# Attention with a feed-forward block: early transfers ahead of constants, batch 1's normalised rows by a SyncE transpose, and one buffer for the last outputs

## The chip, the cores and the metric

The kernel runs on one core of one Trainium2 chip. The metric is the device time of an execution in microseconds; the time of the kernel before is the median of three runs. A core has five engines that work side by side, each with its own queue of instructions in a fixed order: TensorE (PE, matrix products and transposes; PEld is its loading of weights), VectorE (DVE), ScalarE (ACT), GpSimd (POOL) and SyncE (SP, which mainly issues transfers). A transfer (DMA) is issued by an engine's queue, done by 16 shared DMA engines, and lands some microseconds later. An instruction that needs another's result waits on a semaphore, and all that stands behind it in its engine's queue waits with it.

## The reference

```python
scale = 1 / sqrt(D)                                  # B, H, S, D = 8, 8, 576, 64
scores = scale * q @ k.T
cum = cumsum(maximum(s, 0), axis=-1)
bias = -(cum[:, :, :, None] - cum[:, :, None, :])
scores = where(causal, -1e9, scores + minimum(bias, 0))
attn = softmax(scores);  o = attn @ v
x = o.transpose(0, 2, 1, 3).reshape(B, S, H * D)     # (8, 576, 512)
xn = (x - mean(x)) / sqrt(var(x) + 1e-6) * g_ln
out = x + relu(xn @ w_ch1) @ w_ch2                   # 512 -> 2048 -> 512
```

Every batch goes through causal attention with a bias made of running sums, a normalisation of its rows, and a feed-forward block (MLP) whose result is added to the attention's.

## The kernel before

**Tiles.** The 576 rows of a batch are four row tiles of 128 and a tail of 64 (NF = 4, NT = 5, TL = 64). The bias is carried by four more rows beside the 64 of q and k (KA = 68), which hold the running sums in three bf16 pieces (c3). The tails of two batches share one tile (xm, xnm, xTm) and are multiplied at the very end of the kernel (mixed_units).

**Order.** The whole kernel is scheduled by hand: instructions stand on each engine in the order in which the Python code emits them. The string PLAN (L942) lists steps by name (table STEPS) for heads 0 to 17; a loop (L973) emits heads 18 to 63. Batch 0 goes tile by tile (tile_tr T, tile_evac e, tile_scores S, tile_pv V, tile_norm N); later heads by scores (s), scores_d (d), pv (v), pv_norm (n). A head number runs over all batches: head 8 is the first of batch 1, head 18 the third of batch 2. Between the attention's steps, units of an earlier batch's MLP are taken from `queue` by run_units (U and u in the PLAN): mlp1 (one block of 128 hidden columns: four products into ph, then a relu into hT) and mlp2 (a quarter of a row tile: four products into py, and after the fourth quarter yo = py · rstd + x and the output's transfer). run_units(n, True) has the relu of its first unit on VectorE, the others go to ScalarE. The PSUM pool ps_m, with two buffers, holds trt, ph and py; yo lies in a pool of three (yop).

**Inputs.** The layouts of q and k are made in three ways. Batch 0: row tiles loaded by GpSimd's queue with a cast to bf16 (ld_cast_tile, L148) and transposed on TensorE (T). Groups of two heads, called pairs 4 to 11 (heads 8 to 23): ld_cast_pair (L152) loads kp and qp, tr_kind (L276, Q.k.g and Q.q.g in the PLAN) transposes them on TensorE, evac_half (E) copies them to kq. From head 24 on: rows are loaded by SyncE (ld_rows, L170), cast by GpSimd (cast_rows, L178) and transposed by a SyncE transfer (tr_rows, L188). aug (L212, L214) writes the bias rows of a kq buffer with four small SyncE transfers. v is loaded with a cast by GpSimd's queue (ld_cast_v, L160) into v_bf[0] or v_bf[1], by the batch's parity; beside a head's 64 columns each buffer has a column of ones, which gives the softmax's sum. The weights come in four chunks each (ld_w1 L200, ld_w2 L203).

**GpSimd's queue at the start.** It holds, in this order (L638 to L682): ident and maskT; k, q and v of tile 1 with gb (the norm's gain) behind them, of tiles 2 and 3, v of tile 3; w1 chunk 0; pair 4; the tails' k, q and v; constants of kq[2]; w1 chunk 1; constants of v_bf and er, among them the ones columns of v_bf[1] (L666, L667); pair 5; w1 chunk 2; two constants of cT; the five v loads of batch 1; pair 6; w1 chunk 3; w2 chunk 0; pairs 7 and 8; w2 chunk 1. A load that GpSimd issues also waits until the eighth before it has landed. Behind these come w2 chunks 2 and 3 and the causal selects (L346) of heads 10 and up.

**Normalisation and transposition.** ln_xn(b, t) (step l) makes xn of a row tile on VectorE, and with a batch's last tile also rstd. The MLP needs xn transposed (xT). For batches 0 and 1, ln_tr (L527) does this by four TensorE transposes for each tile and a copy from PSUM. From batch 2 on, ln_tr_dma does it with one SyncE transposing transfer for the four full tiles (L516) and one for the tail tile (L512). In the loop, `end` is the head after which the next batch's units enter the queue, and the number of units per head is spread over what remains.

**Which lines matter.** The stalls in the prediction are read at L276 (transposes of pairs), L539 (mlp1), L547 (a relu on VectorE), L557 (mlp2), L566 (yo).

Of the kernel before, what the change touches and what calls it, by code (L numbers as in the profile page):

```python
# [19 lines left out]
def kernel(  # L20
# [11 lines left out]
    nc = tc.nc  # L32
    B, H, S, D = q.shape
# [14 lines left out]
    NG = BH // G  # L48
    NPE = 6
    NM = 10  # L50
    NXD = 2
    KT = 96
    QT = 6
    QP = S // QT
# [99 lines left out]
    def ld_cast_pair(g):  # L154
        ld_cast("k", g)
        ld_cast("q", g)

    def ld_cast_v(b, t):
        pn = P if t < NF else TL
        nc.gpsimd.dma_start(  # L160
            out=v_bf[b % 2][:pn, t, :, 0:D],
            in_=v[b, :, t * P : t * P + pn, :].rearrange("h s d -> s h d"),
        )
# [34 lines left out]
    def ld_w1(c):  # L198
        sl = slice(c * 512, (c + 1) * 512)
        nc.gpsimd.dma_start(out=w1_bf[:, :, sl], in_=w1_r[:, :, sl])  # L200
# [272 lines left out]
    def ln_xn(b, t):  # L473
        tiles = x_tiles(b)
        if t >= len(tiles):
            return
        if b == 0:
            nc.vector.tensor_scalar(
                out=mean0[:, t : t + 1],
                in0=sum0[:, t, 0:1],  # L480
                scalar1=sum0[:, t, 1:2],
                scalar2=1.0 / Dm,
                op0=ALU.add,
                op1=ALU.mult,
            )
# [16 lines left out]
        xns[b, t] = xn  # L502
        if b > 0 and t == len(tiles) - 1:
            ln_rstd(b)
# [44 lines left out]
            nc.scalar.activation(out=hT[:, fb, :], in_=ph, func=ACT.Relu)  # L549

    py = {}

    def mlp2(t, quarter, x, rs, dst, c0=0, c1=512):
        if quarter == 0:
            py[t] = ps_m.tile([P, Dm], F32, name="py", tag="m")[:, 0 : c1 - c0]
        for fb in range(quarter * 4, quarter * 4 + 4):
            nc.tensor.matmul(  # L557
                py[t],
                lhsT=hT[:, fb, t * P : (t + 1) * P],
                rhs=w2_bf[:, fb, c0:c1],  # L560
                start=(fb == 0),
                stop=(fb == FB - 1),
            )
        if quarter == 3:
            yo = yop.tile([P, Dm], F32, name="yo", tag="yo")[:, 0 : c1 - c0]
            nc.vector.scalar_tensor_tensor(  # L566
                out=yo, in0=py[t], scalar=rs, in1=x[:, c0:c1], op0=ALU.mult, op1=ALU.add
            )
            dst(yo, c0, c1)
# [48 lines left out]
    )  # L618
    nc.sync.dma_start(out=c_in, in_=s.rearrange("b h s -> (b h) s"))
    ld_tile("k", 0, nc.sync)  # L620

    nc.vector.memset(zeros.bitcast(F32), 0.0)
    nc.vector.memset(warm, 0.0)
# [5 lines left out]
    nc.vector.memset(rowb[:, :, H : 2 * H, D + 1 : KA], 1.0)  # L629
    nc.vector.memset(v_bf[0][:, 0:NF, :, D : D + 1], 1.0)  # L630
    nc.vector.memset(v_bf[0][0:TL, NF, :, D : D + 1], 1.0)
    for i in range(2):
        nc.vector.memset(kq[i][0:KA, 0, :, S:SP], 0.0)
    nc.vector.memset(eight, 1.0 / scale)
    nc.vector.memset(mhalf, -0.5)
    nc.vector.memset(c3[BH:KT], 0.0)
    nc.vector.memset(rowb[TL:KT, NF], 0.0)
    make_identity(nc, ident)  # L638
    nc.gpsimd.memset(maskT, 0.0)
    nc.gpsimd.affine_select(  # L640
        out=maskT,
        in_=maskT,
        compare_op=ALU.is_ge,
        fill=-1.0e30,
        base=0,
        pattern=[[1, P]],
        channel_multiplier=-1,
    )
    for t in range(1, NF):
        ld_cast_tile("k", t)  # L650
        ld_cast_tile("q", t)
        ld_cast_v(0, t - 1)
        if t == 1:
            nc.gpsimd.dma_start(out=gb, in_=moe_g_ln.partition_broadcast(P))
    ld_cast_v(0, NF - 1)
    ld_w1(0)
    ld_cast_pair(4)
    ld_cast_tile("k", NF)
    ld_cast_tile("q", NF)
    ld_cast_v(0, NF)  # L660

    nc.gpsimd.memset(kq[2][:, :, :, S:SP], 0.0)
    for u, two in ((0, -1.0058441162109375), (1, 1.0019378662109375)):
        nc.gpsimd.memset(kq[2][D:P, u].bitcast(F32)[:, :, 0 : S // 2], two)  # L664
    ld_w1(1)
    nc.gpsimd.memset(v_bf[1][:, 0:NF, :, D : D + 1], 1.0)  # L666
    nc.gpsimd.memset(v_bf[1][0:TL, NF, :, D : D + 1], 1.0)  # L667
    for i in range(2):
        nc.gpsimd.memset(v_bf[i][TL:P, NF, :, :], 0.0)
    nc.gpsimd.memset(er[:, :, OD:EW], 0.0)  # L670
    ld_cast_pair(5)
    ld_w1(2)
    nc.gpsimd.memset(cT[:, :, 0, :, 0], -1.0)
    nc.gpsimd.memset(cT[:, :, 1, :, 1:4], 1.0)
    for t in range(NT):
        ld_cast_v(1, t)
    ld_cast_pair(6)
    ld_w1(3)
    ld_w2(0)
    ld_cast_pair(7)  # L680
# [200 lines left out]
    def pv_next():  # L881
        pb, ph_ = pend.pop(0)
        pv(pb, ph_)
        pv_norm(pb, ph_)
        if ph_ in (3, 5, 7):
            ln_stats(pb, ph_ // 2 - 1)
        if ph_ == 7:
            ln_open(pb)
# [24 lines left out]
        "M": piece,  # L913
        "r": piece_relu,
        "W": lambda n: keep_warm(n),
        "Sk": last_scores,
        "xk": last_exp,
        "relur": lambda: nc.scalar.activation(
# [21 lines left out]
    }  # L940

    PLAN = """  # L942
        relu.0 scan.0 relur hi.0 scan.1 sub.0 hi.1 ck sub.1 mid.0 W.4 mid.1 lo.0 tc.0 bc.0 W.2
        cq T.0.0 scan.2 lo.1 hi.2 e.0.0:D T.0.1 W.2 e.0.1:D sub.2 tc.1 S.0.0.0 x.0.0.0 S.0.1.0
        bc.1 V.0.0 T.1.1 mid.2 N.0.0 x.0.1.0 T.1.0 V.0.1 e.1.1:D S.1.1.0 lo.2 e.1.0:A tc.2 bc.2
# [27 lines left out]
    for n in range(2 * H + 2, BH):  # L973
        b, h = n // H, n % H
        pre(n)

        end = next(m for m in [8 * i + (3 if i <= NXD else 4) for i in range(2, B)] + [BH + 3] if m >= n)
        nu = -(-len(queue) // (end - n + 1)) - 2
        if h % G == 0 and n > 4 * NPE:
            run_units(2)  # L980
            nu -= 2
        scores(b, h)
        run_units(1, True)
        if h % 2 == 0:
            scores_d(b, h // 2)
        post(n)
        run_units(1)
        pv_next()
        pend.append((b, h))
        if b <= NXD:  # L990
            if n == 2 * H + 2:
                for t in range(3, NT):
                    ln_xn(1, t)
            for t in {1: (0, 1, 2), 2: (3, 4)}.get(h, ()) if b > 2 else ():
                ln_xn(b - 1, t)
                if t in (1, 2, 4):
                    run_units(1)
                    nu -= 1
            for t in {2: (0, 1), 3: (2, 3, 4)}.get(h, ()):
                ln_tr(b - 1, t, "act" if b == 2 else "dve")  # L1000
                if t not in (1, 4) and nu > 0:
                    run_units(1)
                    nu -= 1
# [12 lines left out]
        if n == end:  # L1016
            run_units(len(queue))
            queue += batch_units(b - 1)
# [42 lines left out]
```

## Time and profile before

| what | value |
| --- | --- |
| median of three runs | 353.77 us (353.52, 353.77, 355.91) |
| profiled execution, its own time | 354.29 us |
| span of the profiled execution | 352.6 us, 8239 instructions |
| granted TensorE clock | 1.0 |
| TensorE busy | 344.4 us, 98% of the span |
| VectorE, ScalarE, GpSimd busy | 192.2, 190.4, 162.0 us |
| chain that ended last | TensorE 81%, DMA 7%, GpSimd 6% |
| HBM traffic | 37.11 MB read, 9.44 MB written |

The span is what the profiler saw from the first instruction to the last; the execution's own time is 1.7 us longer. In a timeline a row has the start, the duration, the engine, the line of the code, the operation with its tiles (out<-in) and how many instructions the row sums up. A bracket at its end tells how long the engine was idle before it, and whose event ended that. In the page's slices each digit is the busy share of a fortieth of the span, in tenths. In a list of transfers the last number is the median time from issue to landing.

### The profile page before, as it was taken

The numbers are of one execution on the slowest core, as the hardware profiler recorded it, in microseconds if no ns is written. First come the engines' busy times: TensorE is split into PE (matmuls) and PEld (weight loads), VectorE is DVE, ScalarE is ACT, GpSimd is POOL, SyncE is SP. The second block draws the span as 40 slices with busy tenths as digits, with TensorE's granted clock in tenths as the row PEclk, the third lists the DMA queues.
The fourth block names the chain that finished last, engine by engine and source line by source line (L and its number), as shares of the span: only waits on it lengthen the run. The fifth ranks groups of instructions, "written<-read, shape, count | busy, mean of one in ns | idle before, by whom it ended". The sixth has DMA issues, their size and how long they took to land.

```text
span 352.6 us, 8239 instructions
## 1 busy us (share of the span) xinstructions
PE 344.4 (98%) x3110; PEld 196.1 (56%) x3110; DVE 192.2 (55%) x519; ACT 190.4 (54%) x365; POOL 162.0 (46%) x334
## 2 busy tenths in 40 slices
PE   7999999999999999999999999999999999999995
PEld 3898666655555555555555555555555544444444
DVE  7788688964366537562655458443844582113112
ACT  4799798977635673367526662576347403402500
POOL 9996587284455736383756365445521010000000
PEclk9999999999999999999999999999999999999999
DMA  9999999899998999999999999999830033011012
GB/s 150 170 164 150 201 204 129 144 176 143 187 188 132 196 210 178 210 198 176 188 199 205 198 180 171 203 160 200 148 108 0 3 81 112 2 59 59 3 41 79
DMA packets 169160, 50.31 MB, mean 143 GB/s; under 512 B 156896, under 2 KB 164512, under 8 KB 169120
## 3 DMA queue, kind: packets, MB, share of 16 engines
q1 hardware_dynamic: 115168, 36.54, 56.0%
q0 software_dynamic: 52432, 12.46, 41.1%
q10 hardware_dynamic: 1520, 0.79, 0.9%
q8 instruction: 24, 0.39, 0.5%
q14 instruction: 16, 0.13, 0.1%
HBM read 37.11 MB, written 9.44 MB: 132 GB/s over the span
## 4 chain that ended last, share of the span: by engine, by line
PE 81%; DMA 7%; POOL 6%; DVE 2%; issue 1%; SPq 1%; POOLq 0%; DVEq 0%
PE ph L539 32%; PE py L557 32%; PE pot L404 7%; DMA w_bf<-in_moe_w_ch_dram 5%; PE sc L326 3%; PE sb L326 3%; PE sa L326 3%; POOL rowb L148 2%; DMA rowtmp<-in_q_dram 2%; POOL v_bf L160 1%; PE trqk L276 1%; DMA out_dram<-yo 1%; DVE yo L566 1%; SPq L170 1%; POOL kq L664 1%
## 5 line engine op out<-in xcount | busy, mean ns | idle before, releaser
L557 PE MATMUL py<-w_bf,hT 128*128 128x512 bf16 (+2 forms) x608 | 133.6, 368 | 0.0
L539 PE MATMUL ph<-xT,w_bf 128*128 128x512 bf16 x480 | 112.5, 379 | 0.7 <-DMA w_bf<-in_moe_w_ch_dram 0.7
L549 ACT ACTIVATE hT<-ph 128x512 bf16<-128x512 f32 x102 | 60.8, 598 | 73.2 <-PE ph L539 73.2
L557 PEld LDWEIGHTS <-hT 128*128 128x128 bf16 x608 | 54.3, 98 | 52.7
L539 PEld LDWEIGHTS <-w_bf 128*128 128x128 bf16 x544 | 49.5, 98 | 51.3 <-issue 0.8
L337 ACT ACTIVATE er<-sa 128x512 bf16<-128x512 f32 x56 | 33.4, 597 | 59.4 <-PE sa L326 53.0
L346 POOL TENSOR_SCALAR_AFFINE_SELECT er<-er 128x256 bf16<-128x256 bf16 x108 | 44.3, 430 | 35.5 <-ACT er L337 34.7
L547 DVE TENSOR_SCALAR hT<-ph 128x512 bf16<-128x512 f32 x34 | 23.5, 692 | 58.0 <-PE ph L539 50.0
L566 DVE SCALAR_TENSOR_TENSOR yo<-py,rstd,xb 128x512 f32<-128x512 f32 x32 | 23.9, 748 | 35.8 <-PE py L557 34.5
L404 PEld LDWEIGHTS <-er 128*128 128x128 bf16 x840 | 32.9, 98 | 13.1 <-POOL er L346 0.9
L326 PEld LDWEIGHTS <-kq 68*128 68x128 bf16 x400 | 28.5, 97 | 19.8
L160 POOL DMA_DIRECT2D v_bf<-in_v_dram x40 | 34.6, 872 | 2.5 <-PE pot L404 1.8
L404 PE MATMUL pot<-v_bf,er 128*128 128x65 bf16 x840 | 34.9, 194 | 0.4 <-POOL er L346 0.4
L337 ACT ACTIVATE er<-sc 128x512 bf16<-128x512 f32 x56 | 34.1, 610 | 0.0
L337 ACT ACTIVATE er<-sb 128x512 bf16<-128x512 f32 x56 | 33.5, 597 | 0.0
L178 POOL CAST rowb<-rowtmp 128x512 bf16<-128x512 f32 (+1 forms) x25 | 15.3, 610 | 34.4 <-DMA rowtmp<-in_k_dram 14.9
L416 DVE RECIPROCAL rinv<-pot 128x5 f32<-128x5 f32 x56 | 10.8, 192 | 36.9 <-PE pot L404 36.8
L178 POOL CAST kq<-rowtmp 128x512 bf16<-128x512 f32 (+1 forms) x25 | 15.4, 616 | 30.9 <-DMA rowtmp<-in_q_dram 27.5
L418 DVE TENSOR_TENSOR xb<-pot,rinv 128x256 f32<-128x256 f32 x56 | 23.8, 425 | 1.9
L494 DVE SCALAR_TENSOR_TENSOR xn<-xb,mv,gb 128x512 bf16<-128x512 f32 x28 | 22.9, 818 | 1.0
L448 DVE BATCH_NORM_STATS2 stats<-xb 128x6 f32<-128x128 f32 (+1 forms) x84 | 21.9, 320 | 0.3
L326 PE MATMUL sc<-kq 68*128 68x256 bf16 (+1 forms) x192 | 21.7, 228 | 0.0
(118 smaller groups left out, 354.4 us busy)
## 6 DMA issues: line engine op xcount, KB each, us to landing
out_dram<-yo SPq DMA_DIRECT2D x32, 256.0 KB
rowtmp<-in_k_dram SPq DMA_DIRECT2D x40, 128.0 KB
rowtmp<-in_q_dram SPq DMA_DIRECT2D x40, 128.0 KB
v_bf<-in_v_dram POOLq DMA_DIRECT2D x32, 128.0 KB, 5.6
w_bf<-in_moe_w_ch_dram POOLq DMA_DIRECT2D x8, 512.0 KB, 9.7
kp<-in_k_dram POOLq DMA_DIRECT2D x8, 144.0 KB, 7.9
qp<-in_q_dram POOLq DMA_DIRECT2D x8, 144.0 KB, 7.9
rowtmp<-in_k_dram SPq DMA_DIRECT2D x10, 64.0 KB
```

Source lines behind the costliest of these rows:

```text
L160: nc.gpsimd.dma_start(out=v_bf[b % 2][:pn, t, :, 0:D], in_=v[b, :, t * P : t * P + pn, :].rearrange("h s d -> s h d"),)
L178: nc.gpsimd.tensor_copy(out=rows[gam % 2][0:pn, t, :, :, 0:D], in_=loaded.pop(("rows", gam, t))[0:pn])
L326: nc.tensor.matmul(a[:, c + a0 - q0 : c + a1 - q0], lhsT=k_cols(b, h, kb), rhs=cols, start=True, stop=not (pe_mask and diag),)
L337: nc.scalar.activation(out=e[:, o : o + 512], in_=a, func=ACT.Exp, scale=scale)
L346: nc.gpsimd.affine_select(out=two, in_=two, compare_op=ALU.is_ge, fill=0.0, base=0, pattern=[[0, 2], [1, P]], channel_multiplier=-1,)
L404: nc.tensor.matmul(pot[:, t, :], lhsT=e[:, o : o + P], rhs=vv[:, kb, h, :], start=(kb == 0), stop=(kb == last),)
L418: nc.vector.tensor_tensor(out=xb[b][:, :, hs], in0=pot[:, 0:NF, 0:D], in1=rinv[:, 0:NF].unsqueeze(2).to_broadcast([P, NF, D]), op=ALU.mult,)
L539: nc.tensor.matmul(ph, lhsT=w1_bf[:, kd, fb * P : (fb + 1) * P], rhs=xT[:, :, kd, :], start=(kd == 0), stop=(kd == KD - 1),)
L547: nc.vector.tensor_scalar_max(out=hT[:, fb, :], in0=ph, scalar1=0.0)
L549: nc.scalar.activation(out=hT[:, fb, :], in_=ph, func=ACT.Relu)
L557: nc.tensor.matmul(py[t], lhsT=hT[:, fb, t * P : (t + 1) * P], rhs=w2_bf[:, fb, c0:c1], start=(fb == 0), stop=(fb == FB - 1),)
L566: nc.vector.scalar_tensor_tensor(out=yo, in0=py[t], scalar=rs, in1=x[:, c0:c1], op0=ALU.mult, op1=ALU.add)
```

## The change

It has four parts.

- The head of the program. On GpSimd the loads of k, q and v of tile 1 stand ahead of ident, and those of tile 2 ahead of maskT. gb is loaded by SyncE, behind c_in and k of tile 0. Four memsets leave VectorE's head (two of kq go to GpSimd; mhalf and rowb's tail come later, step m). GpSimd's constants and loads are reordered: w1 chunk 1 directly behind the tails' loads, pair 5 between two memsets of kq[2], w1 chunk 2 ahead of v_bf's constants, and the two memsets of v_bf[1]'s ones columns behind the five v loads of batch 1. In the PLAN's first lines, cq comes earlier, and mid.0 and lo.0 come ahead of sub.1.
- Batch 1's transposes. The PLAN ends with l.3 and D, which is ln_tr_dma(1, 0): one SyncE transposing transfer for the four full tiles, in place of 16 TensorE transposes and four ScalarE copies. The tail tile is normalised at head 19 and transposed by SyncE at head 20, in place of four transposes and a copy.
- The first units of batch 1. At head 20 (`late`), the two units that the loop has around the scores come behind PV of head 18, together.
- The last outputs. The last mixed tile is multiplied in three column pieces (256, 128, 128). Each piece had a yo buffer of its own; now the three share one buffer, yos[t], at their own columns.

The diff, with unchanged lines mostly left out:

```diff
     def mlp2(t, quarter, x, rs, dst, c0=0, c1=512):
...
-            yo = yop.tile([P, Dm], F32, name="yo", tag="yo")[:, 0 : c1 - c0]
+            if c0 == 0:
+                yos[t] = yop.tile([P, Dm], F32, name="yo", tag="yo")
+            yo = yos[t][:, c0:c1]
...
     ld_tile("k", 0, nc.sync)
+    nc.sync.dma_start(out=gb, in_=moe_g_ln.partition_broadcast(P))
...
-    for i in range(2):
-        nc.vector.memset(kq[i][0:KA, 0, :, S:SP], 0.0)
     nc.vector.memset(eight, 1.0 / scale)
-    nc.vector.memset(mhalf, -0.5)
     nc.vector.memset(c3[BH:KT], 0.0)
-    nc.vector.memset(rowb[TL:KT, NF], 0.0)
-    make_identity(nc, ident)
-    nc.gpsimd.memset(maskT, 0.0)
-    nc.gpsimd.affine_select(
...
     for t in range(1, NF):
         ld_cast_tile("k", t)
         ld_cast_tile("q", t)
         ld_cast_v(0, t - 1)
         if t == 1:
-            nc.gpsimd.dma_start(out=gb, in_=moe_g_ln.partition_broadcast(P))
+            make_identity(nc, ident)
+        if t == 2:
+            nc.gpsimd.memset(maskT, 0.0)
+            nc.gpsimd.affine_select(
...
     ld_cast_v(0, NF)
-
+    ld_w1(1)
+    for i in range(2):
+        nc.gpsimd.memset(kq[i][0:KA, 0, :, S:SP], 0.0)
     nc.gpsimd.memset(kq[2][:, :, :, S:SP], 0.0)
+    ld_cast_pair(5)
     for u, two in ((0, -1.0058441162109375), (1, 1.0019378662109375)):
         nc.gpsimd.memset(kq[2][D:P, u].bitcast(F32)[:, :, 0 : S // 2], two)
-    ld_w1(1)
+    ld_w1(2)
+    for i in range(2):
+        nc.gpsimd.memset(v_bf[i][TL:P, NF, :, :], 0.0)
+    for t in range(NT):
+        ld_cast_v(1, t)
+    nc.gpsimd.memset(er[:, :, OD:EW], 0.0)
     nc.gpsimd.memset(v_bf[1][:, 0:NF, :, D : D + 1], 1.0)
     nc.gpsimd.memset(v_bf[1][0:TL, NF, :, D : D + 1], 1.0)
-    for i in range(2):
-        nc.gpsimd.memset(v_bf[i][TL:P, NF, :, :], 0.0)
-    nc.gpsimd.memset(er[:, :, OD:EW], 0.0)
-    ld_cast_pair(5)
-    ld_w1(2)
+    ld_cast_pair(6)
     nc.gpsimd.memset(cT[:, :, 0, :, 0], -1.0)
     nc.gpsimd.memset(cT[:, :, 1, :, 1:4], 1.0)
-    for t in range(NT):
-        ld_cast_v(1, t)
-    ld_cast_pair(6)
     ld_w1(3)
     ld_w2(0)
     ld_cast_pair(7)
...
+        "m": lambda: (nc.vector.memset(rowb[TL:KT, NF], 0.0), nc.vector.memset(mhalf, -0.5)),
+        "D": lambda: ln_tr_dma(1, 0),
...
     PLAN = """
-        relu.0 scan.0 relur hi.0 scan.1 sub.0 hi.1 ck sub.1 mid.0 W.4 mid.1 lo.0 tc.0 bc.0 W.2
-        cq T.0.0 scan.2 lo.1 hi.2 ...
+        relu.0 scan.0 relur cq hi.0 scan.1 sub.0 hi.1 ck mid.0 lo.0 W.4 sub.1 mid.1 tc.0 bc.0 W.2
+        T.0.0 scan.2 lo.1 hi.2 ...
...
-        l.2 E.q.11.0:A E.q.11.1:A l.1
+        l.2 E.q.11.0:A E.q.11.1:A l.1 l.3 D
...
-        end = next(m for m in [8 * i + (3 if i <= NXD else 4) for i in range(2, B)] + [BH + 3] if m >= n)
+        end = next(m for m in [8 * i + (3 if i == 2 else 4) for i in range(2, B)] + [BH + 3] if m >= n)
...
         scores(b, h)
-        run_units(1, True)
+        late = n == 2 * H + 4
+        run_units(0 if late else 1, True)
         if h % 2 == 0:
             scores_d(b, h // 2)
         post(n)
-        run_units(1)
+        run_units(0 if late else 1)
         pv_next()
+        run_units(2 if late else 0, True)
         pend.append((b, h))
-        if b <= NXD:
-            if n == 2 * H + 2:
-                for t in range(3, NT):
-                    ln_xn(1, t)
...
-            for t in {2: (0, 1), 3: (2, 3, 4)}.get(h, ()):
-                ln_tr(b - 1, t, "act" if b == 2 else "dve")
...
-        elif h in XN_AT:
+        if h in XN_AT and n > 2 * H + 2:
             for t in XN_AT[h][0]:
                 ln_xn(b - 1, t)
```

More of the change, by code (lines that the diff above doesn't have):

```diff
@@ L50 @@
     NM = 10
-    NXD = 2
     KT = 96
@@ L551 @@
     py = {}
+    yos = {}
     def mlp2(t, quarter, x, rs, dst, c0=0, c1=512):
@@ L631 @@
     nc.vector.memset(v_bf[0][0:TL, NF, :, D : D + 1], 1.0)
-    for i in range(2):
-        nc.vector.memset(kq[i][0:KA, 0, :, S:SP], 0.0)
     nc.vector.memset(eight, 1.0 / scale)
-    nc.vector.memset(mhalf, -0.5)
     nc.vector.memset(c3[BH:KT], 0.0)
-    nc.vector.memset(rowb[TL:KT, NF], 0.0)
-    make_identity(nc, ident)
-    nc.gpsimd.memset(maskT, 0.0)
-    nc.gpsimd.affine_select(
[L641 to L648, printed above, removed]
     for t in range(1, NF):
@@ L653 @@
         if t == 1:
-            nc.gpsimd.dma_start(out=gb, in_=moe_g_ln.partition_broadcast(P))
+            make_identity(nc, ident)
+        if t == 2:
+            nc.gpsimd.memset(maskT, 0.0)
+            nc.gpsimd.affine_select(
+                out=maskT,
+                in_=maskT,
+                compare_op=ALU.is_ge,
+                fill=-1.0e30,
+                base=0,
+                pattern=[[1, P]],
+                channel_multiplier=-1,
+            )
     ld_cast_v(0, NF - 1)
@@ L942 @@
     PLAN = """
-        relu.0 scan.0 relur hi.0 scan.1 sub.0 hi.1 ck sub.1 mid.0 W.4 mid.1 lo.0 tc.0 bc.0 W.2
-        cq T.0.0 scan.2 lo.1 hi.2 e.0.0:D T.0.1 W.2 e.0.1:D sub.2 tc.1 S.0.0.0 x.0.0.0 S.0.1.0
-        bc.1 V.0.0 T.1.1 mid.2 N.0.0 x.0.1.0 T.1.0 V.0.1 e.1.1:D S.1.1.0 lo.2 e.1.0:A tc.2 bc.2
+        relu.0 scan.0 relur cq hi.0 scan.1 sub.0 hi.1 ck mid.0 lo.0 W.4 sub.1 mid.1 tc.0 bc.0 W.2
+        T.0.0 scan.2 lo.1 hi.2 e.0.0:D T.0.1 W.2 e.0.1:D sub.2 tc.1 S.0.0.0 x.0.0.0 S.0.1.0
+        bc.1 V.0.0 T.1.1 mid.2 N.0.0 x.0.1.0 T.1.0 V.0.1 e.1.1:D S.1.1.0 lo.2 m e.1.0:A tc.2 bc.2
         x.1.1.0 S.1.0.0 T.2.0 S.1.1.1 bc.4 T.2.1 e.2.0:D x.1.0.0 S.1.0.1 x.1.1.1 S.2.0.0 T.3.0
@@ L986 @@
         post(n)
-        run_units(1)
+        run_units(0 if late else 1)
         pv_next()
+        run_units(2 if late else 0, True)
         pend.append((b, h))
-        if b <= NXD:
-            if n == 2 * H + 2:
-                for t in range(3, NT):
-                    ln_xn(1, t)
[L994 to L998, printed above, removed]
-            for t in {2: (0, 1), 3: (2, 3, 4)}.get(h, ()):
-                ln_tr(b - 1, t, "act" if b == 2 else "dve")
-                if t not in (1, 4) and nu > 0:
-                    run_units(1)
-                    nu -= 1
-        elif h in XN_AT:
+        if h in XN_AT and n > 2 * H + 2:
             for t in XN_AT[h][0]:
```

## The prediction

> **What bounds the kernel now.** I read the page first: share by engine, slices, chain of waits. Then I followed TensorE, GpSimd and the transfers in the timeline, stretch by stretch, where the change works: 0 to 50 us, 66 to 80 us and the last 9 us.
>
> ```profile
> PE 344.4 (98%) x3110; PEld 196.1 (56%) x3110; DVE 192.2 (55%) x519; ACT 190.4 (54%) x365; POOL 162.0 (46%) x334
> ...
> PE   7999999999999999999999999999999999999995
> ...
> PE 81%; DMA 7%; POOL 6%; DVE 2%; issue 1%; SPq 1%; POOLq 0%; DVEq 0%
> ```
>
> TensorE (PE) is busy in every slice but the first and the last, at a granted clock of 1.0. An idle microsecond, or one of matmuls taken away, therefore moves the end by a microsecond; other engines count only where they make PE wait. The next lines are TensorE's timeline: the places where the change can do that first.
>
> ```profile
> 39.43 1.02 PE L539 MATMUL ph<-xT,w_bf 128*128 128x512 bf16 x4 [0.73 <-DMA w_bf<-in_moe_w_ch_dram]
> 40.29 0.42 PE L276 MATMUL trqk<-ident,qp 96*128 96x96 bf16 x6
> ...
> 46.17 0.42 PE L276 MATMUL trqk<-ident,kp 96*128 96x96 bf16 x6
> 46.43 0.42 PE L276 MATMUL trqk<-ident,qp 96*128 96x96 bf16 x6
> ```
>
> These are the last real stall (0.73 us) and the first uses of qp6 (40.29), kp7 (46.17) and qp7 (46.43), each a load that GpSimd issues.
>
> **GpSimd's queue (the large term).** Both programs have two short memsets that write the ones column of v_bf[1], batch 1's v. Before, they stand ahead of the five loads of that buffer and wait for nothing. In the changed order they stand behind these loads, write the same buffer, and the program makes them wait until all five have landed. Queued behind them on GpSimd are pair 6, two memsets of cT, w1 chunk 3, w2 chunk 0, pairs 7 and 8, w2 chunk 1, head 10's selects and w2 chunks 2 and 3. GpSimd's timeline before:
>
> ```profile
> 18.88 0.25 POOL L666 MEMSET v_bf<- 128x32 bf16 x1
> 18.93 0.22 POOL L667 MEMSET v_bf<- 64x8 bf16 x1
> ...
> 22.76 0.85 POOL L673 MEMSET cT<- 128x320 bf16 x1
> 23.37 1.04 POOL L674 MEMSET cT<- 128x960 bf16 x1
> 24.32 4.23 POOL L160 DMA_DIRECT2D v_bf<-in_v_dram  x5
> 28.48 0.71 POOL L152 DMA_DIRECT2D kp<-in_k_dram  x1
> 29.11 0.71 POOL L152 DMA_DIRECT2D qp<-in_q_dram  x1
> 31.05 0.79 POOL L200 DMA_DIRECT2D w_bf<-in_moe_w_ch_dram  x1 [1.23 <-DMA w_bf<-in_moe_w_ch_dram]
> 32.25 0.74 POOL L203 DMA_DIRECT2D w_bf<-in_moe_w_ch_dram  x1 [0.41 <-DMA v_bf<-in_v_dram]
> 33.74 0.64 POOL L152 DMA_DIRECT2D kp<-in_k_dram  x1 [0.75 <-DMA v_bf<-in_v_dram]
> 35.47 0.64 POOL L152 DMA_DIRECT2D qp<-in_q_dram  x1 [1.08 <-DMA v_bf<-in_v_dram]
> ```
>
> When do the five loads land? The DMA view by window gives issue to landing; the first line is for the fifth load (issued at 27.8), the others for w1 chunk 3 with w2 chunk 0, and pair 7:
>
> ```profile
> v_bf<-in_v_dram POOLq DMA_DIRECT2D x1, 64.0 KB, 9.4
> ...
> w_bf<-in_moe_w_ch_dram POOLq DMA_DIRECT2D x2, 512.0 KB, 10.1
> kp<-in_k_dram POOLq DMA_DIRECT2D x1, 144.0 KB, 9.9
> qp<-in_q_dram POOLq DMA_DIRECT2D x1, 144.0 KB, 8.9
> ```
>
> So L, the landing of the last v tile, is 27.8 + 9.4 = 37.2 us before. The page's DMA slices stand at 8 or 9 tenths up to 60 us: the transfers are bound by their engines, and an earlier issue does not land them earlier, while the bytes ahead of these five loads are the same. Afterwards nothing is queued behind the v tiles, so a slow engine may finish sooner; the landings of v tiles 2 and 3 in the trace (35.2, 36.6) less about a microsecond give a lower end of 34.3. I take L = 36.5.
>
> From L on: the two memsets take about 0.3 us, kp6's issue 0.64, qp6's starts at L + 0.95, the cT memsets take 1.65 (22.76 to 24.41), and w1(3) is issued at about L + 3.2, w2(0) at L + 3.95, kp7 at L + 4.7, qp7 at L + 5.3. Two uses are endangered. qp6: its load then takes no less than the lightest v load of the trace (3.7, at 58.8) and no more than a pair's load at 53.2 (5.2), so it lands at L + 4.65 to L + 6.15, and is late for 40.29 by L − 35.6 to L − 34.1: 0.9 to 2.4 us at L = 36.5. Pair 7: the queue restarts empty. The first packet of a load comes 1.7 to 2.0 us after its issue in this trace, so w1(3) starts at L + 5.0; weight chunks land 2.5 to 2.7 us apart and pair loads 0.5 to 0.9 apart here, so the two chunks, kp7 and qp7 need 2 × 2.6 + 2 × 0.7, and a last microsecond to the semaphore: kp7 lands near L + 12, qp7 between L + 12.7 and, with the spread of up to 2 us between the trace's DMA engines, L + 14.5. Against 46.43, qp7 is late by L − 33.7 to L − 31.9. The lower end is 0.6 (L = 34.3), the upper 5.3 (L = 37.2, slow engine). I take **+3.5 us**, 49.9 for qp7, in the lower half since two transfers can overlap. This counts once: the stall at qp6 is part of it, because pair 7 has an absolute time. V of head 8 (37.19) waits for the memset too, and aug(2), which SyncE now issues near 22 instead of 18.1, may be late for head 8's scores at 27.99; both stalls come before pair 7 and vanish in the same 3.5 unless they are larger. w1(3) itself, used at 45.10, lands near L + 8.9 = 45.4 and is covered by the same stall; pair 8, w2(1) to w2(3) and head 10's selects have slack behind it.
>
> [...]
>
> **The start.** The k, q and v loads of the first tiles are issued ahead of ident and maskT. VectorE sheds four memsets, of them rowb's tail (0.51) directly ahead of the first relu at 4.38, which can start at 3.87. TensorE's first transposes of tile 0 (7.65) come up to 0.75 earlier; 0 if k0's landing decides. Moving gb's load to SyncE's queue, behind c_in and k0 and ahead of the aug loads, spares GpSimd 0.6 us of issue. Price: 0 to −0.75, and I count **0**, since pair 7's clock does not move with it. It is what the stall hides; without the stall it counts in full.
>
> **Batch 1's transposes.** Five groups of four on TensorE and five ScalarE copies (0.59 each) leave.
>
> ```profile
> L527 PE MATMUL trx<-ident,xn x32: 217/219/222, 18.6 to 74.5; 128*128 128x128 bf16 x32
> ...
> L516 SPq DMA_TRANSPOSE xT<-xn x6: 1329/1820/3014, 107.9 to 287.5; - x6
> ```
>
> The second line is the same transposition for later batches: 1.3 to 3.0 us of issue, and 4.3 to 7.3 us from issue to landing in the trace. On TensorE, four cost 0.22 us of the path (74.29 to 74.51), so 20 give −1.1. The last row tile's norm, xn(3), is now ready near 70.4 (a 0.95 us step after l.1 ends at 69.43), the transpose issued at 70.45 lands at 74.8 (77.7 at worst). The first unit of batch 1, now behind PV of head 18, would want it at 75.39 − 1.1 + 0.5 = 74.8: just met. But both first units now come together and the third needs a buffer that VectorE empties, behind a yo of 0.75 (74.49), the normalisation of head 18 and a relu of 0.69: about 0.6 us of stall. Net **−0.5**; −1.1 without stalls, +1.8 with the slowest landing (2.9 late, less 1.1). On SyncE the transpose goes ahead of one output and six row loads, which move back by its 1.6 us; their casts and the transposes for head 24 (landed by 90, used at 93.1) have about 3 us of slack, so nothing there. The second transpose, xTm's, is needed only at the end of the kernel. ScalarE's copies were not on the path: 0.
>
> **The last outputs.** VectorE's timeline of the end:
>
> ```profile
> 347.40 0.35 DVE L566 SCALAR_TENSOR_TENSOR yo<-py,rstd,xm 128x128 f32<-128x128 f32 x1 [0.41 <-PE py L557]
> 348.73 0.35 DVE L566 SCALAR_TENSOR_TENSOR yo<-py,rstd,xm 128x128 f32<-128x128 f32 x1 [0.98 <-PE py L557]
> ```
>
> The idle time of 0.98 is put down to TensorE, but the chain of waits ends with 2.64 us of out_dram<-yo (345.55 to 348.19): the last piece waits for a buffer whose output is still under way. In one buffer that wait is gone. The other pieces start 0.26 us after their last matmul; at that, the last starts at 348.30: **−0.4**.
>
> **Sum**: +3.5 + 0 − 0.5 − 0.4 = +2.6 on the profiled execution's 354.29 (span 352.6 and 1.7 around it), 356.9. That execution lies 0.52 above the median of the runs, so on 353.77: **356.4 us**.
>
> **Rivals.** First, *the hold ends early*: the five v tiles land by L = 33.4 (46.43 less 13), or pair 7 comes as fast as the lone loads (3.7 to 5.2 us), so that no use is late. Then the start counts: −0.7 − 0.5 − 0.4 = −1.6, 352.2 us. For it: an earlier start of the queue by a microsecond, and no load behind the v tiles. Against: landings of 35 to 37 before, with full engines. Second, *the restart of the queue costs all it can*, slower by over 1%: one slow DMA engine delays qp7 beyond 46.43 + 3.54 + 0.9 = 50.9 us, and the transposes at 46.43 wait that long. At L = 37.2 and L + 14.5 the stall is 5.3 and the time 358.2. For it: weight chunks took 10.0 to 12.0 us to landing at 38 to 41 us. Against: fewer loads are in flight. Third, that the change does not do what it says: v_bf's memsets might have been put down to another dependency, or SyncE's transpose collide with the loads; then the batch-1 term is +1.8 and the hold 0, 355.2, inside the forecast's range.
>
> **How the numbers follow.** Forecast, 54%: its own range is 352.9 (0.6 − 1.1 − 0.4) to 357.3. Early end, 16%: 352.2. Full price, 30%: 357.3 to 359.2. About 1%, 3.54 us, is what a measurement of this kernel can tell from no change. Slower by more is the full price, 0.30; faster by more is beyond every term and gets 0.02; within it, 0.68. The range is 351.9 to 359.2: a little below the early end, and above the full price by a microsecond for a late transpose of batch 1.
>
> **What would show it.** GpSimd's memset of v_bf should show an idle time of several microseconds, ended by v_bf's DMA; TensorE's transposes of qp or kp a stall at 40 to 50 us that sums to 2 to 5 us; the first hT of batch 1 a gap of some 0.6; TensorE's trx transposes a count of 16 instead of 36; the last yo an idle time near 0.5 instead of 0.98. If no transpose waits on kp or qp between 38 and 52 us, the hold is wrong and with it the sign; if pair 7 is in time and TensorE still stalls there, I have the wrong load.

## The result, and the profile after

The changed kernel takes 356.17 us (median of 17 runs, 354.0 to 358.95), the kernel before 354.13 in the same comparison (17 runs). The ratio is 1.0056, 95% interval 1.0035 to 1.0077: slower by 2.0 us, a little over half a per cent. The forecast was 356.4. The profiled execution took 356.63 us, its span is 354.9, and the granted clock 1.0.

Where TensorE waits in the changed kernel is told by the list of waits of the trace; its columns are the line that waited, what ended the wait, microseconds in total, how often, and the longest:

```profile
PE ph L538 <- DMA xT<-xn: 1.5, 1, 1.5
...
PE sa L325 <- POOL er L672: 1.1, 1, 1.1
PE pot L776 <- ACT er L735: 0.9, 1, 0.9
PE trqk L275 <- DMA kp<-in_k_dram: 0.7, 1, 0.7
PE trqk L275 <- DMA qp<-in_q_dram: 0.4, 1, 0.4
```

Behind the first 8 us, the kernel before had, above 0.32 us, one wait of 0.73 (ahead of the products at 39.43) and one of 0.37 (at 120). Neither is left; the five shown here are new. Two of the releasers are not what they seem: er's memset (L672) had ended at 28.86 when head 8's scores began at 29.51, but the last of kq[2]'s bias rows landed at 29.2; and the first product with v began at 10.64, just behind v's first tile, which landed at 10.51 (8.87 before). By these times both waits are for transfers.

The predicted hold is plain in GpSimd's timeline of the changed kernel:

```profile
34.48 0.25 POOL L673 MEMSET v_bf<- 128x32 bf16 x1 [5.62 <-DMA v_bf<-in_v_dram]
34.56 0.20 POOL L674 MEMSET v_bf<- 64x8 bf16 x1
35.00 0.65 POOL L151 DMA_DIRECT2D kp<-in_k_dram  x1 [0.24 <-issue]
35.63 0.64 POOL L151 DMA_DIRECT2D qp<-in_q_dram  x1
...
37.83 0.81 POOL L199 DMA_DIRECT2D w_bf<-in_moe_w_ch_dram  x1
38.61 0.78 POOL L202 DMA_DIRECT2D w_bf<-in_moe_w_ch_dram  x1
39.34 0.68 POOL L151 DMA_DIRECT2D kp<-in_k_dram  x1
39.98 0.68 POOL L151 DMA_DIRECT2D qp<-in_q_dram  x1
```

GpSimd idles 5.62 us. The loads behind it are issued up to 6.8 us later than before (w1 chunk 3 at 37.83 instead of 31.05), and pair 7 is late, as TensorE's timeline shows:

```profile
40.84 0.42 PE L275 MATMUL trqk<-ident,qp 96*128 96x96 bf16 x6
...
47.63 0.43 PE L275 MATMUL trqk<-ident,kp 96*128 96x96 bf16 x6 [0.75 <-DMA kp<-in_k_dram]
48.42 0.43 PE L275 MATMUL trqk<-ident,qp 96*128 96x96 bf16 x6 [0.36 <-DMA qp<-in_q_dram]
```

Batch 1's transposes are gone from TensorE (16 of 36 are left), but SyncE's queue, first in the changed kernel, then in the kernel before, tells what came for them:

```profile
72.40 1.90 SPq L515 DMA_TRANSPOSE xT<-xn  x1
74.41 1.06 SPq L586 DMA_DIRECT2D out_dram<-yo  x1
...
81.42 6.89 SPq L187 DMA_TRANSPOSE kq<-kq  x3
...
90.96 3.08 SPq L511 DMA_TRANSPOSE xTm<-xnm  x1
...
99.10 6.65 SPq L187 DMA_TRANSPOSE kq<-rowb  x3
...
111.18 3.15 SPq L515 DMA_TRANSPOSE xT<-xn  x1
```

```profile
70.12 0.36 SPq L584 DMA_DIRECT2D out_dram<-yo  x1
...
75.81 8.90 SPq L188 DMA_TRANSPOSE kq<-kq  x3
...
93.79 6.57 SPq L188 DMA_TRANSPOSE kq<-rowb  x3
...
107.93 1.33 SPq L516 DMA_TRANSPOSE xT<-xn  x1
```

Batch 1's transpose waits in the queue for xn until 72.40, so that the output behind it is issued 4.3 us later and the transposes for head 24 5.6 us later. By 88.4, ahead of xTm's transpose, the queue is still 3.6 us behind. The transposes of head 28's rows are issued 5.3 us later and batch 2's xT 3.25 us later, although TensorE is only 1.2 to 1.4 us later there. At the end the last piece no longer waits for an output. VectorE's timeline:

```profile
350.42 0.35 DVE L568 SCALAR_TENSOR_TENSOR yo<-py,rstd,xm 128x128 f32<-128x128 f32 x1 [0.41 <-PE py L557]
351.31 0.35 DVE L568 SCALAR_TENSOR_TENSOR yo<-py,rstd,xm 128x128 f32<-128x128 f32 x1 [0.54 <-PE py L557]
```

The idle time ahead of the last yo is 0.54 instead of 0.98. The time lost can be followed by subtracting the start of the same TensorE or VectorE work in the two timelines:

| work | before | after | behind by |
| --- | --- | --- | --- |
| first transposes of tile 0 | 7.65 | 6.97 | −0.68 |
| first product with v | 10.51 | 10.64 | +0.13 |
| scores of head 8 | 27.99 | 29.51 | +1.52 |
| transposes of qp6 | 40.29 | 40.84 | +0.55 |
| transposes of qp7 | 46.43 | 48.42 | +1.99 |
| scores of head 20 | 74.73 | 75.62 | +0.89 |
| first unit of batch 2 | 113.37 | 116.45 | +3.08 |
| last piece but one | 347.40 | 350.42 | +3.02 |
| last piece | 348.73 | 351.31 | +2.58 |

### The profile page after: what moved, and what is told of

Same layout as the page of the kernel before. It is cut to its first block, busy times and chain, and to the rows that moved or that the text cites. A ratio compares the mean times of both kernels' runs of the same rounds, so it can differ in the third digit from the quotient of the medians.

```text
span 354.9 us, 8170 instructions
## 1 busy us (share of the span) xinstructions
PE 342.9 (97%) x3066; PEld 195.0 (55%) x3090; DVE 192.4 (54%) x517; ACT 188.1 (53%) x360; POOL 161.7 (46%) x335
## 4 chain that ended last, share of the span: by engine, by line
PE 80%; DMA 8%; POOL 6%; DVE 2%; issue 2%; ACT 0%; POOLq 0%; ACTq 0%
PE py L557 33%; PE ph L538 31%; PE pot L403 7%; PE sb L325 3%; PE sa L325 3%; PE sc L325 3%; DMA qp<-in_q_dram 2%; DMA w_bf<-in_moe_w_ch_dram 2%; DMA v_bf<-in_v_dram 2%; POOL v_bf L159 2%; DMA xT<-xn 1%; POOL rowb L147 1%; PE trqk L275 1%; DVE yo L568 1%; DVE xb L417 1%
## 5 line engine op out<-in xcount | busy, mean ns | idle before, releaser
L557 PE MATMUL py<-w_bf,hT 128*128 128x512 bf16 (+2 forms) x584 | 130.9, 367 | 1.3
L336 ACT ACTIVATE er<-sa 128x512 bf16<-128x512 f32 x56 | 33.4, 597 | 63.2 <-PE sa L325 58.1
L325 PEld LDWEIGHTS <-kq 68*128 68x128 bf16 x400 | 28.5, 97 | 21.5 <-POOL er L672 1.2
L159 POOL DMA_DIRECT2D v_bf<-in_v_dram x40 | 34.3, 861 | 4.0 <-DMA w_bf<-in_moe_w_ch_dram 2.0
L325 PE MATMUL sa<-kq 68*128 68x512 bf16 x56 | 21.3, 381 | 1.1 <-POOL er L672 1.1
```

The source lines that it names most:

```text
L159: nc.gpsimd.dma_start(out=v_bf[b % 2][:pn, t, :, 0:D], in_=v[b, :, t * P : t * P + pn, :].rearrange("h s d -> s h d"),)
L325: nc.tensor.matmul(a[:, c + a0 - q0 : c + a1 - q0], lhsT=k_cols(b, h, kb), rhs=cols, start=True, stop=not (pe_mask and diag),)
L336: nc.scalar.activation(out=e[:, o : o + 512], in_=a, func=ACT.Exp, scale=scale)
L557: nc.tensor.matmul(py[t], lhsT=hT[:, fb, t * P : (t + 1) * P], rhs=w2_bf[:, fb, c0:c1], start=(fb == 0), stop=(fb == FB - 1),)
```

## The experiments

Differences of a few tenths lie inside the spread of the runs (before: 352.5 to 358.1 over all comparisons), so medians decide from about a microsecond up, and single waits are read in the traces. Ratios are against the kernel before in the same comparison.

**The hold, taken out and put in.** a1_ones_first is the changed kernel with this edit:

```diff
+    nc.gpsimd.memset(v_bf[1][:, 0:NF, :, D : D + 1], 1.0)
+    nc.gpsimd.memset(v_bf[1][0:TL, NF, :, D : D + 1], 1.0)
     for t in range(NT):
         ld_cast_v(1, t)
     nc.gpsimd.memset(er[:, :, OD:EW], 0.0)
-    nc.gpsimd.memset(v_bf[1][:, 0:NF, :, D : D + 1], 1.0)
-    nc.gpsimd.memset(v_bf[1][0:TL, NF, :, D : D + 1], 1.0)
```

> The changed kernel, with the two memsets of v_bf[1]'s ones columns put ahead of the five v loads of batch 1; nothing else is undone. Theory (the memsets' wait holds GpSimd's queue and delays pair 7): the 5.6 us idle time of GpSimd goes, kp7 and qp7 are in time, the 0.75 and 0.36 us ahead of the transposes at 47.6 and 48.4 us go, and the time falls by 1 to 1.5 us, to about 355.0. Rival (transfers are late because the DMA engines are full, whoever issues them): the same stall stays and the time stays at 356.2. Second rival (what is won at pair 7 is lost at the transpose of batch 2's rows, whose queue runs on its own time): the stall at 48 us goes, the stall ahead of batch 2's first unit grows from 1.5 to 2.5 us or more, and the time stays near 356.2.

Measured: 354.82 us, ratio 1.0014 (0.9988 to 1.0039), down from 1.0056. No wait on kp or qp is left. Its waits:

```profile
PE pot L776 <- DMA v_bf<-in_v_dram: 1.2, 1, 1.2
PE sa L325 <- DMA kq<-c: 1.1, 1, 1.1
PE pot L403 <- POOL er L345: 1.0, 2, 0.8
```

So the hold is worth some 1.5 us of the changed kernel's 2.0, as the theory had it (the two intervals just touch); both rivals fall. In the traces, 1.1 us of it stands at qp7 (47.32 here, 48.42 in the changed kernel). Here the profile names the two transfers behind the early waits, v's first tile and the bias rows.

b1_ones_late is the opposite: the kernel before, with only these two lines moved behind the loads.

> The kernel before, with only the two memsets of v_bf[1]'s ones columns moved behind the five v loads of batch 1. Theory: GpSimd idles some 5 us until the v tiles land near 35, qp7 lands some 14 us after that, 2 to 3 us late for 46.4, and the time rises by 1.5 to 2.5 us, to about 356. Rival (the hold alone costs nothing, since the 0.73 us stall at 38.5 us and the slack at pair 7 take it): 354.1 and no stall of TensorE on kp or qp between 38 and 52 us.

Measured: 358.04 us (354.98 to 359.67), ratio 1.0101 (1.0068 to 1.0134). That is more than the whole change costs, and more than the theory's 356. The profiled execution was the fastest of the six, 354.98. Its memset idles 5.32 us, and the wait of 0.73 us at 38.5 us is gone; two of its waits:

```profile
PE trqk L276 <- DMA kp<-in_k_dram: 1.4, 1, 1.4
...
PE trqk L276 <- DMA qp<-in_q_dram: 0.3, 1, 0.3
```

TensorE is 1.06 us behind at qp7 (47.49 against 46.43), which fits 354.98 but not 358. The runs differ in one more thing, the mean granted clock: 1.0 and 0.999 in the two runs below 357, 0.990 to 0.995 in the four of 358 to 359.7. a2_xtm_late, told below, caught it in a profile: a hold with a wait of 2.28 us for kp7 and 0.38 for qp7. Its windows, with the granted clock in the column behind the engines (third number from the end), and TensorE's busy time as the second number:

```profile
46.00:48.00 2.00, 1.02 (x5) 0.29 (x3) 1.20 (x3) 1.66 (x4) 1.86 (x5) 1.00 1.21 187
48.00:50.00 2.00, 0.43 (x6) 0.28 (x6) 0.23 (x1) 0.00 (x0) 1.91 (x5) 0.97 1.30 198
50.00:52.00 2.00, 1.89 (x24) 1.61 (x25) 0.89 (x3) 1.18 (x2) 1.55 (x4) 0.50 1.26 206
52.00:54.00 2.00, 2.00 (x9) 0.83 (x7) 1.74 (x6) 1.97 (x4) 1.18 (x2) 0.50 1.22 202
54.00:56.00 2.00, 2.00 (x19) 1.23 (x18) 0.52 (x2) 0.62 (x2) 1.43 (x3) 0.50 1.24 205
56.00:58.00 2.00, 2.00 (x13) 1.00 (x12) 0.39 (x2) 0.99 (x3) 0.00 (x0) 0.82 1.26 205
```

Behind the first of the two waits TensorE runs at half clock for 6.8 us, and loses an estimated 3.4. In b1_ones_late a mean clock of 0.995 stands for an estimated 1.7 us lost and 0.990 for 3.5. That is about half to three quarters of what its four slower runs take beyond 354.98. They left no trace, and that the rest is longer waits for pair 7 is not shown.

**The clock, tested by itself.** Three copies of the kernel before have a wait put in far from the change, in the last batch; k is 1, 4 or 8:

```diff
                 nc.sync.dma_start(out=out[b, t * P : (t + 1) * P, c0:c1], in_=yo)
+                if (b, t) == (B - 1, 1):
+                    for _ in range(k):
+                        nc.vector.memset(zeros.bitcast(F32), 0.0)
+                    keep_warm(1)
```

> The kernel before, with a wait put into TensorE's order far from the change, in the last batch's second product (row tile 1 to row tile 2, near 313.7 us): one idle product of 512 columns that waits until VectorE has done yo of that tile and one more memset of 0.25 us. TensorE waits about 1.2 us. Theory (waits of about 1.9 us and more, not shorter ones, are followed by some microseconds at half clock): granted clock 1.0 in all slices, and 353.9 + 1.2 + 0.2 = 355.3. Rival (the clock falls for other reasons, the wait has no part in it): the same 355.3.

> As c1_wait_short, with four memsets in place of one: TensorE waits about 2.0 us. Theory: in part of the runs the clock falls to 0.5 for some 3.4 us behind the wait, which costs 1.7 more; runs near 356.1 and runs near 357.8, with a granted clock of 1.0 and of 0.995. Rival: the time grows with the wait alone, 356.1 in all runs.

> As c1_wait_short, with eight memsets in place of one: TensorE waits about 3.0 us. Theory: the clock falls to 0.5 for 3.4 to 7 us behind the wait in nearly all runs, and the median is 357.1 + 1.7 to 3.4, that is 358.8 to 360.5, granted clock 0.99 to 0.995. Rival: 357.1.

The waits in the profiles are 1.12, 2.30 and 3.86 us, the last two longer than planned. The medians are 355.13, 357.69 and 360.72, the ratios 1.0040 (1.0009 to 1.0070), 1.0093 (1.0066 to 1.0121) and 1.0162 (1.0119 to 1.0206). With the short wait, 11 of 12 runs keep a mean clock of 0.997 or more, and the cost, 1.0, is the wait. With the middle one the runs part into two kinds: six with a clock of at least 0.998 (median 357.09) and six with 0.995 (median 358.47). With the long one all six lie at 0.988 to 0.995; the wait alone would give 354.1 + 3.9 + 0.2 = 358.2. The windows of c3_wait_long behind its wait:

```profile
313.00:317.00 4.00, 0.14 (x2) 0.08 (x2) 2.93 (x9) 0.00 (x0) 0.00 (x0) 1.00 0.17 66
317.00:321.00 4.00, 4.00 (x12) 1.44 (x13) 0.00 (x0) 0.00 (x0) 0.00 (x0) 0.57 0.00 0
321.00:325.00 4.00, 3.95 (x19) 1.85 (x19) 0.75 (x1) 0.00 (x0) 0.00 (x0) 1.00 0.17 66
```

The theory holds, the rival falls: the clock fell behind one idle stretch of 2.3 us in six runs of twelve, and behind one of 3.9 in all six. A mean clock of 0.995 is half clock for 3.4 us in a span of 353, an estimated 1.7 us lost; the two kinds of runs with the middle wait lie 1.4 apart, and the long wait's median 2.5 above the wait alone.

b1_filled tries to cover the hold of b1_ones_late with work:

```diff
-        ... s.12 U u
+        ... s.12 U u W.10
         Q.k.7 Q.q.7
```

> The kernel before with the two memsets of v_bf[1] behind the five v loads, as in b1_ones_late, and with ten idle products of 512 columns (0.216 us each, 2.2 us in all) on TensorE just ahead of the transposes of kp7; they compute nothing that is used. Theory (a wait of TensorE of some two microseconds, not its length alone, is what costs: the granted clock falls to half for 6 to 7 us after it): the products fill the wait, the clock stays at 1.0 and the median falls from 358.0 to about 356, although work is added. Rival (b1_ones_late's median comes from longer waits for pair 7): the median stays at 358 or rises, and a wait of a microsecond or more still stands behind the products.

Measured: 357.91 us, ratio 1.0121 (1.0085 to 1.0156). The expected fall did not come. In the four runs with a clock of at least 0.998 the median is 357.6, so the clock held in most runs. The filler, an estimated 2.2 us by 0.216 for each product, runs in full whether pair 7 is late or not; what else kept the time up is not shown. The profiled execution ran at a clock of 0.95 from start to end, so its durations are not used; its order of events shows kp7 landing as the filler ends. That filling a wait pays is not shown.

**SyncE's queue.** b2_batch1 is the kernel before with only batch 1's part of the change (l.3 and D in the PLAN, `late`, the tail by SyncE).

> The kernel before with only batch 1's part: l.3 and one SyncE transpose at the PLAN's end, the tail tile by SyncE at head 20, the first two units behind PV of head 18. Theory (SyncE's queue is now full and delays the transpose of batch 2's rows): 1.1 us of TensorE transposes go, about 0.3 come back at the third unit, and TensorE stalls 1 to 1.5 us ahead of batch 2's first unit near 113 us; the time is within 0.5 us of before, 353.8 to 354.6. Rival (that stall comes from the delays of the first 50 us and not from SyncE's queue): no such stall, and 353.3.

Measured: 353.49 us, ratio 0.9980 (0.9957 to 1.0002). No wait stands ahead of batch 2's first unit, and 0.25 at batch 1's third unit; the rival's 353.3 is the better number, and the theory that SyncE's transposes alone make that wait falls: it takes the delays of the changed kernel's start as well. But the margin shrank: xT lands 0.77 us ahead of its use (111.83 for 112.60), 1.12 before (112.25 for 113.37).

a2_xtm_late is the changed kernel with one transpose moved:

```diff
             for t in XN_AT[h][1]:
-                ln_tr_dma(b - 1, t)
+                if n != 2 * H + 4:
+                    ln_tr_dma(b - 1, t)
+            if n == 3 * H + 4:
+                ln_tr_dma(1, NF)
```

> The changed kernel with one SyncE instruction moved: the transpose of batch 1's tail tile (xTm) is issued at head 28, behind that of batch 2's rows, instead of head 20. Theory (its 3.1 us on SyncE's queue near 91 us delay all that follows there): the rows of head 28 and batch 2's transpose are issued up to 3 us earlier, the 1.5 us stall ahead of batch 2's first unit shrinks below 0.4, and the time falls by about 1.2 us, to 355.0. Rival (the first transpose or the earlier stalls have delayed SyncE, not xTm's): the stall stays above 1 us and the time at 356.2.

Measured: 356.08 us, ratio 1.0069 (1.0040 to 1.0098). The wait ahead of batch 2's first unit is gone from the profile, xT 0.95 ahead. The time did not follow: the hold is still there, and in four of seven runs the mean clock is 0.989 to 0.995 (median 356.7, the others 355.6). For time this run is inconclusive; a6_gb_sp below has the same edit without the hold.

**The early transfers.** a3_aug_early is a1_ones_first with kq[2]'s memsets earlier:

```diff
-    ld_w1(1)
     for i in range(2):
         nc.gpsimd.memset(kq[i][0:KA, 0, :, S:SP], 0.0)
     nc.gpsimd.memset(kq[2][:, :, :, S:SP], 0.0)
-    ld_cast_pair(5)
     for u, two in ((0, -1.0058441162109375), (1, 1.0019378662109375)):
         nc.gpsimd.memset(kq[2][D:P, u].bitcast(F32)[:, :, 0 : S // 2], two)
+    ld_w1(1)
+    ld_cast_pair(5)
```

> a1_ones_first, with GpSimd's memsets of kq[2] ahead of w1 chunk 1 and pair 5, as in the kernel before. Theory (head 8's scores wait for the bias rows of kq[2], whose transfers are issued 4.3 us later because SyncE waits for the last of these memsets): the 1.1 us of idle time ahead of head 8's scores go and the time falls by about 1 us, to 353.9. Rival (the DMA engines are full and the small transfers land late whenever they are issued; or the time is given back at a later transfer): the stall stays above 0.7, or the median stays at 354.8.

Measured: 353.91 us, ratio 0.9980 (0.9963 to 0.9996), and head 8's scores wait for nothing. The theory holds in the trace; the step from a1's ratio (0.9988 to 1.0039) is near the noise. The wait for xT is back in this profile, 1.2 us.

a4_gb_back is a1_ones_first with gb's load in GpSimd's queue, behind v of tile 0:

```diff
-    nc.sync.dma_start(out=gb, in_=moe_g_ln.partition_broadcast(P))
...
         if t == 1:
+            nc.gpsimd.dma_start(out=gb, in_=moe_g_ln.partition_broadcast(P))
             make_identity(nc, ident)
```

> a1_ones_first, with gb's load back in GpSimd's queue, behind k, q and v of tile 1 and 0. Theory (gb on SyncE's queue runs beside these loads and lets v's first tile land at 10.5 instead of 8.9): v lands before 9.5, the 0.9 to 1.4 us wait of TensorE ahead of its first product with v (9.6 us) falls below 0.5, and the start's 0.7 us stay won at 12 us; the median falls by 0.5 to 1, if no later transfer takes it back. Rival (the early loads of GpSimd collide with q and k of tile 0 themselves): v lands after 10 all the same.

Measured: 356.62 us, ratio 1.0057 (1.0030 to 1.0085): slower than a1. The first half of the theory holds: v lands at 8.83 and its first product starts at 10.04, with 0.22 of wait. In the five traces with gb on SyncE (the changed kernel, a1, a2, a3, a6) v lands at 10.5 to 11.3, in five with gb behind it (before, a4, a5, b1, b2) at 8.8 to 9.1. But the microsecond won is waited for at the bias rows, which land no earlier: head 8's scores wait 1.96 us instead of 1.08 and start at 29.88, where a1 has 29.85. Then the clock falls. The windows of a4_gb_back:

```profile
28.00:30.00 2.00, 0.12 (x1) 0.13 (x2) 1.93 (x6) 0.55 (x1) 2.00 (x4) 1.00 2.25 159
30.00:32.00 2.00, 1.91 (x37) 1.58 (x36) 0.12 (x1) 1.57 (x3) 2.00 (x4) 0.98 2.60 153
32.00:34.00 2.00, 2.00 (x25) 2.00 (x22) 0.42 (x1) 1.97 (x4) 2.00 (x4) 0.50 2.74 89
34.00:36.00 2.00, 2.00 (x28) 2.00 (x26) 1.02 (x2) 1.08 (x3) 1.32 (x3) 0.66 1.30 146
```

Two of its twelve runs kept a clock of 0.998 or more, and took 353.1 and 353.3; the ten others 354.9 to 359.3. At the transposes of qp7 a4 is 1.6 us behind a1 (48.95 against 47.32), which is about what half clock for 3.4 us costs (an estimated 1.7): in this profile the earlier start made the kernel slower, because it turned a wait of 1.1 into one of 2.0. The profile has a second stretch of half clock from 124.1 us, behind a wait of 1.78 us for a GpSimd select; why this wait was longer than a1's 0.75 is not shown.

**All repairs.** a5_all joins the edits of a1, a2, a3 and a4; a6_gb_sp is the same with gb on SyncE as in the change, so it is a3 with a2's edit.

> The changed kernel with all four repairs: ones memsets ahead of the v loads, kq[2]'s memsets ahead of w1 chunk 1 and pair 5, gb's load in GpSimd's queue, batch 1's tail transpose at head 28. Theory: none of the stalls at 9.6, 28, 47 and 115 us is left; what the change takes away remains: 0.7 at the start, 0.8 net of batch 1's transposes and 0.4 at the end, so 352.0, below the kernel before (353.9) by 0.5%. Rival (the transfers of the first 60 us bound the start, and what is won early is waited for at a later load): a stall on a load of kp, qp, w_bf or v_bf of 1 us or more between 20 and 60 us, and 353 or above.

> a5_all with one repair left out: gb is loaded by SyncE ahead of tile 1's k, q and v, as in the changed kernel. It parts the two edits by which a5_all differs from a3_aug_early (353.91 against 352.27). Theory (gb beside these loads delays v of tile 0, and xTm's transpose at head 20 delays batch 2's): TensorE waits 1.2 to 1.5 us at 9.5 us for v's first tile, the wait ahead of batch 2's first unit near 112 us stays below 0.3, and the time lies between, near 353.2. Rival (one of the two does it all): 353.9 if gb does it, 352.3 if the transpose does.

Measured: a5_all 352.27 us, ratio 0.9954 (0.9940 to 0.9969); a6_gb_sp 352.76 us, ratio 0.9952 (0.9927 to 0.9977). Both beat the kernel before by half a per cent, and no run of either has a clock below 0.998. The waits of a5_all, without the one ahead of TensorE's first instruction:

```profile
PE pot L403 <- POOL er L345: 0.3, 1, 0.3
PE st L718 <- DVE kq L110: 0.3, 1, 0.3
PE pot L403 <- POOL er L375: 0.3, 1, 0.3
```

gb's place makes no difference to the time that these runs can show: in a6 v lands late again (10.51), but TensorE waits 0.45 us there, not the 1.2 to 1.5 expected. Moving xTm's transpose from head 20 to head 28 does show in the traces: xT, late by 1.1 in a3 (113.52 for 112.41), lands 1.2 ahead of its use in a6 (110.72 for 111.92). The ratios, 0.9980 for a3 and 0.9952 for a6, point the same way, but their intervals overlap. Over the traces, xT's margin is −1.4, −1.1, 0.0, +0.1 and +0.8 with xTm at head 20 (the changed kernel, a3, a1, a4, b2), and +0.9 to +1.2 where it is later or not on SyncE (a2, a5, a6, before).

## Why the prediction was right, point by point

- **The sum** came out: +2.6 forecast, +2.3 in the profiled executions, +2.0 by the medians. Two of its terms were off by about 1.5 us in opposite directions, so the agreement of the total is in part luck.
- **The hold** was the right mechanism at the right place, shown from both sides by a1 and b1. Its size was over-estimated: 3.5 against 1.99 at qp7. The term at fault is L: the last v tile landed at 34.51 (27.55 + 6.96), not 36.5, close to the lower end of 34.3. That nothing was queued behind it is the reason, as b1 shows: with only the memsets moved, L falls from 37.23 to 33.75. From L on, the working held: qp7 issued at L + 5.5 (forecast 5.3), landed at L + 13.9 (12.7 to 14.5). qp6, which at L = 36.5 would have been late, landed in time, at L + 4.9 (4.65 to 6.15). The "spread of up to 2 us" was read too small: it holds for loads issued before 21.5 us, but for those issued from 24 to 41 us in the kernel before, the first and the last of a load's 16 signals of landing lie 3.3 to 4.9 us apart. In the changed kernel it is 1.0 for pair 7, and the upper bound held. From w1 chunk 3's issue to qp7's landing it was 10.5 us (37.83 to 48.38).
- **The start** was counted at 0, with gain −0.75 where nothing hides it. TensorE did start 0.68 earlier, but lost it within four microseconds at v's first tile, not, as I had written, at pair 7. I had weighed gb's move by the 0.6 us of issue that GpSimd saves, and not by what gb takes from the three loads beside it: 1.6 us.
- **Bias rows (aug).** I named a late aug(2) as a possible stall that would vanish in the hold. The 1.1 us came, and vanished in it by the arithmetic, but stood open once the hold was out (a1 to a3: the wait goes, and the ratio falls by 0.0034, 1.2 us).
- **Batch 1's transposes.** The −1.1 is there (+1.99 at qp7, +0.89 at head 20), the third unit's stall is 0.26 rather than 0.6. The step that failed is SyncE's queue: "about 3 us of slack, so nothing there", and xTm "needed only at the end". Batch 1's first transpose moved what stood behind it back by 4.3 to 5.7 us, not by its 1.6 (in b2, without the late start, the transposes for head 24 by 3.3). xTm's result is needed late, but its issue is not free: it held the queue for 3.08 us, and everything behind it, up to batch 2's transpose, moved back. The wait there, 1.5 us, is the second error. The queue is not all of it: that xT was issued 1.2 us after its xn was ready (111.18 and 109.96; 107.93 and 107.90 before), and landed 5.2 us after its issue instead of 4.3. Why the transfer itself took longer is not shown. With the first 50 us as before (b2) there was no wait, and with xTm's transpose moved (a2, a6) there was none either, so its issue at head 20 was needed for the wait but not enough. Batch 1's own transpose was "just met", as forecast: it landed at 76.82, and its first product began at 76.86.
- **The last outputs**: −0.44 in the traces, −0.4 forecast.
- **Rivals.** The early end did not happen (34.5, not 33.4). The full price, over 357.3, came in one run of the 17: 358.95, with a mean clock of 0.993; four of the 17 had a clock of 0.995 or less. A fall of the clock, which the prediction did not have at all, is therefore part of that run's time; whether a slow DMA engine had a part is not recorded. The third did not happen: the memsets waited for v_bf's loads, as said.

## What to carry to other kernels

A memset into a buffer that loads are filling made its whole engine wait for the loads, 5.62 us here; put such constants ahead of the loads, above all on a queue that also issues transfers. When a transfer is moved, ask both what waits for its result and how long its issue holds the queue for those behind it. A wait has to be priced by its length: those of 1.5 us or less cost themselves here (c1 paid 1.0 us for one of 1.12), and behind those of 1.78, 1.96 and 2.28 us (a4, a2) the granted clock was 0.5 for 3.4 to 6.8 us, an estimated 1.7 to 3.4 more, while behind one of 2.30 (c2) it held in half the runs; so an earlier start that only lengthens the next wait can be a loss.

## What the hardware showed

The half clock behind a wait was not expected. Behind waits of 1.96 and of 1.78 us (a4) the granted clock was 0.5 for 3.4 us each, behind 2.28 and 0.38 (a2) for 6.8. With the wait of 2.30 (c2) the mean clock was 0.995 in six runs of twelve, with that of 3.86 (c3) it was 0.988 to 0.995 in all six. In profiles whose longest wait was 1.5 us or less (before, the changed kernel, a1, a3, a5, a6, b1, b2, c1) the clock stayed at 1.0 there. A fall need not come at once: in a4 the wait ends at 29.88, TensorE goes on at full clock for 2.05 us, and the clock falls at 31.93. What sets the lengths of 3.4 and 6.8 us, and what parts the two kinds of c2's runs, is not shown.

The clock's own records in these traces allow one step more. In a4 the four changes around its two waits lie a whole number of steps of 3.413 us behind the first: by 27.31, 30.72, 119.47 and 122.88 us, which are 8, 9, 35 and 36 steps. The kernel before and the changed kernel have one change each behind the first, after the last product; it comes 348.16 and 351.57 us later, which are 102 and 103 steps. The steps around a4's two waits, and the one that holds most of c2's, counted on from its first change:

```profile
28.52:31.93 3.41, 1.96 (x36) 1.64 (x37) 1.59 (x3) 1.55 (x4) 3.41 (x6) 1.00 2.51 155
31.93:35.34 3.41, 3.41 (x41) 3.41 (x38) 0.80 (x2) 3.10 (x6) 3.12 (x5) 0.50 2.19 101
120.68:124.09 3.41, 1.61 (x23) 0.76 (x21) 1.02 (x2) 1.35 (x4) 3.40 (x9) 1.00 1.05 212
124.09:127.50 3.41, 3.41 (x15) 1.21 (x11) 0.91 (x3) 0.60 (x1) 3.11 (x7) 0.50 1.86 135
...
312.29:315.71 3.42, 1.75 (x9) 0.59 (x6) 1.39 (x4) 0.00 (x0) 0.00 (x0) 1.00 0.21 80
```

Each fall stands at the end of 3.41 us in which TensorE idled for much of the time: 1.45 and 1.80 us here, 2.43 in a2, 2.92 in c3. In c2's profile a border of the steps so counted parts the wait of 2.30 us into 1.67 and 0.63, and the clock held. That the idle time of a step decides is not shown: a fall came behind 1.45 us of it (a4), and none behind 1.48 (the changed kernel) or 1.67 (c2).
